# Linear attention mixed with a GEGLU feed-forward block on one core: K and Q of the first four tiles moved ahead of the feed-forward units, with finer loads at the start

## The chip, the cores and the metric

One core of one Trainium2 chip. The metric is the time of one execution in microseconds (us). Engines: PE is the TensorE matmul, PEld its weight load, DVE the VectorE, ACT the ScalarE, POOL the GpSimd, SP the queue that issues most DMA loads. "Clock" below means the rate at which PE takes columns: a 512-column matmul takes 427 ns while it is slow and 216 ns once it is released (spacing of matmul starts in the traces). "Landed" means that the last update of a load's semaphore has come. A bracket on a row of weight loads is idle time of the weight loads; the time that PE itself stands can be shorter (0.31 against 0.64 us in the first profile of the changed kernel).

## The reference

Two branches read the same `x` (2048 tokens, 640 features) and are mixed by a gate:

```python
g = sigmoid((x * gate_w).sum(-1, keepdims=True))
a = linear_attention(x, wqkv) @ wo      # 32 heads of 20; phi(t) = where(t > 0, t + 1, exp(t)) + 1e-6
b = (gelu(x @ w_gate) * (x @ w_up)) @ w_down   # 1728 hidden features
return g * a + (1 - g) * b
```

## The kernel before

Tokens are cut into 16 tiles of 128 and 4 quarters of 512. `xT` is x with features on the partitions; the first quarter is transposed on PE, the others by DMA. The order is: E (feed-forward units, 14 per quarter) of quarter 0; K of all 16 tiles; Q of all tiles with G (x transposed times phi(K)) between them; then the rest of E and the output F. The PSUM pool has 8 buffers, shared by all.

```python
dma(out=x_sb[0][:, 0:2, :], in_=x_view[:, 0:2, :])       # x tiles 0, 1: 320 KB
dma(out=wg[:, :, 0:256], in_=wg_v[:, :, 0:256])          # 320 KB
dma(out=wu[:, :, 0:256], in_=wu_v[:, :, 0:256])          # 320 KB
dma(out=x_sb[0][:, 2:4, :], in_=x_view[:, 2:4, :])       # x tiles 2, 3: 320 KB
# ... the rest of w_gate and w_up, then w_k, gate_w in 2-byte pieces, transposing loads, w_q ...

for r in range(NWARM):                                    # NWARM = 7
    nc.tensor.matmul(t[:], lhsT=ones, rhs=ones, ...)      # warm-up

transpose_x(0)                                            # tiles 0, 1
e01 = [(ps_tile("ps_g"), ps_tile("ps_u")) for _ in range(2)]
for ft in range(2):
    e_mm(e01[ft][0], wg, ft, 0, 0, 256)                   # half a quarter wide
e_mm(e01[0][1], wu, 0, 0, 0, 256)
transpose_x(1)                                            # tiles 2, 3
e_mm(e01[1][1], wu, 1, 0, 0, 256)
for ft in range(2):
    e_mm(e01[ft][0], wg, ft, 0, 256, 256)
    e_mm(e01[ft][1], wu, ft, 0, 256, 256)
    e_out(0, ft, *e01[ft])
for ft in range(2, NF):
    phase_E(0, ft)
for st in range(NT):
    phase_K(st)
# ... Q with G, and the rest ...
```

Of the kernel before, what the change touches and what calls it, by code (L numbers as in the profile page):

```python
# [16 lines left out]
def kernel(  # L17
# [12 lines left out]
    nc = tc.nc  # L30
# [13 lines left out]
    GW = GH * Dh  # L44
    NG = 6
    gw = [min(GW, D - GW * g) for g in range(NG)]
    NWARM = 7

    x2 = A_x[0]
    out2 = out[0]  # L50
# [8 lines left out]
    def ps_tile(name):  # L59
        return psum.tile([P, QW], FP32, name=name, tag="ps")  # L60
# [7 lines left out]
    x_sb = [x_all[:, 4 * q : 4 * q + 4, :] for q in range(NQ)]  # L68
    pk_q = [ov.tile([P, 4, D], BF16, name=f"pk{q}", tag="slab_a", bufs=NQ) for q in range(NQ)]
    pk = [pk_q[t // 4][:, t % 4, :] for t in range(NT)]  # L70
    WQK = 2 * D + 1
    wqk = ov.tile([P, ND, WQK], BF16, name="wqk", tag="slab_c")

    wg = wpool.tile([P, ND, FM], BF16, name="wg")
    wu = wpool.tile([P, ND, FM], BF16, name="wu")
# [10 lines left out]
    nc.gpsimd.memset(ones_bf[:], 1.0)  # L86

    dma = nc.sync.dma_start
    dma(out=x_sb[0][:, 0:2, :], in_=x_view[:, 0:2, :])  # L89
    dma(out=wg[:, :, 0:256], in_=wg_v[:, :, 0:256])  # L90
    dma(out=wu[:, :, 0:256], in_=wu_v[:, :, 0:256])  # L91
    dma(out=x_sb[0][:, 2:4, :], in_=x_view[:, 2:4, :])
    warm = consts.tile([P, 1], FP32, name="act_warm")
    nc.scalar.activation(out=warm[:], in_=nc.const_aps.tensor(1.0, [P, 1], BF16), func=ACT.Gelu_apprx_tanh)
    for lo, hi in ((256, 512), (512, 1024), (1024, FM)):
        dma(out=wg[:, :, lo:hi], in_=wg_v[:, :, lo:hi])
        dma(out=wu[:, :, lo:hi], in_=wu_v[:, :, lo:hi])
    dma(out=wgu[:, :, 0:FL], in_=wg_v[:, :, FM:F])
    dma(out=wgu[:, :, FL:P], in_=wu_v[:, :, FM:F])
    dma(out=wqk[:, :, 0:D], in_=wqkv_v[:, :, D : 2 * D])  # L100
    with nc.allow_non_contiguous_dma(reason="tiny gate_w column load"):
        dma(out=wqk[:, :, D : D + 1], in_=gate_w.rearrange("(k p o) -> p k o", p=P, o=1))
    for q in (1, 2, 3):
        nc.sync.dma_start_transpose(out=xT[q][:, :, :], in_=x2[q * QW : (q + 1) * QW, :])
    dma(out=wqk[:, :, D + 1 : WQK], in_=wqkv_v[:, :, 0:D])
    for q in (1, 2, 3):
        dma(out=x_sb[q][:], in_=x_view[:, 4 * q : 4 * q + 4, :])
    dma(out=wv[:], in_=wqkv_v[:, :, 2 * D : 3 * D])
# [6 lines left out]
    for r in range(NWARM):  # L115
        nc.tensor.matmul(t[:], lhsT=nc.const_aps.tensor(1.0, [P, P], BF16),
                         rhs=nc.const_aps.tensor(1.0, [P, QW], BF16), start=(r == 0), stop=(r == NWARM - 1))

    NGB = 4
    mask = consts.tile([GW, NGB * GW], BF16, name="mask")  # L120
# [12 lines left out]
    eneg = consts.tile([P, NT], FP32, name="eneg")  # L133
    gsc = {}

    def transpose_x(pair):
        t0 = 2 * pair
        tpa = psum.tile([P, 2 * QW], BF16, name="tp_a", tag="ps")
        tpb = psum.tile([P, 2 * QW], BF16, name="tp_b", tag="ps")
        c0 = t0 * P  # L140
        for dk in range(ND):
            tp, o = (tpa, dk * 2 * P) if dk < 2 else (tpb, (dk - 2) * 2 * P)
            for i in range(2):
                nc.tensor.transpose(  # L144
                    tp[:, o + i * P : o + (i + 1) * P], x_sb[0][:, t0 + i, dk * P : (dk + 1) * P], ident[:]
                )
        nc.vector.tensor_copy(
            out=xT[0][:, 0:2, c0 : c0 + 2 * P], in_=tpa[:, 0 : 4 * P].rearrange("p (k n) -> p k n", k=2),
        )
        nc.scalar.copy(  # L150
            out=xT[0][:, 2:3, c0 : c0 + 2 * P], in_=tpb[:, 0 : 2 * P].rearrange("p (k n) -> p k n", k=1),
        )
        nc.vector.tensor_copy(
            out=xT[0][:, 3:5, c0 : c0 + 2 * P], in_=tpb[:, 2 * P : 6 * P].rearrange("p (k n) -> p k n", k=2),
        )

    hT_cur = {}
    hT0 = big.tile([P, NF, QW], BF16, name="hT0")
# [3 lines left out]
    def e_mm(ps, w, ft, q, t0=0, tw=QW):  # L162
        for dk in range(ND):
            nc.tensor.matmul(ps[:, t0 : t0 + tw], lhsT=w[:, dk, ft * P : (ft + 1) * P],  # L164
                             rhs=xT[q][:, dk, t0 : t0 + tw], start=(dk == 0), stop=(dk == ND - 1))

    def e_out(q, ft, psg, psu):
        gl = work.tile([P, QW], BF16, name="gl")
        nc.scalar.activation(out=gl[:], in_=psg[:], func=ACT.Gelu_apprx_tanh)  # L169
        nc.vector.tensor_tensor(out=hT_cur[q][:, ft, :], in0=psu[:], in1=gl[:], op=ALU.mult)  # L170
# [24 lines left out]
            out=dst, in0=src, scalar=0.0, in1=m[:, :width], op0=ALU.max, op1=ALU.add,  # L195
        )

    def proj(ps, st, lo, hi):
        q, sl = divmod(st, 4)
        for dk in range(ND):  # L200
            nc.tensor.matmul(  # L201
                ps[:, 0 : hi - lo], lhsT=xT[q][:, dk, sl * P : (sl + 1) * P],
                rhs=wqk[:, dk, lo:hi], start=(dk == 0), stop=(dk == ND - 1),
            )

    CH = ((0, QW), (QW, D))

    def phase_K(st):
        for lo, hi in CH:
            ps = ps_tile("ps_k")  # L210
            proj(ps, st, lo, hi + (hi == D))
            phi(pk[st][:, lo:hi], ps[:, 0 : hi - lo], hi - lo)
        nc.scalar.activation(
            out=eneg[:, st : st + 1], in_=ps[:, D - QW : D - QW + 1], func=ACT.Exp, scale=-1.0
        )

    def phase_Q(st):
        for lo, hi in CH:
            ps = ps_tile("ps_q")
            proj(ps, st, D + 1 + lo, D + 1 + hi)  # L220
            phi(pq[st][:, lo:hi], ps[:, 0 : hi - lo], hi - lo)

    g_sb = big.tile([P, ND, D], BF16, name="g_sb")
# [19 lines left out]
    def phase_Z(st):  # L243
        if st == 0:
            return
        nc.vector.tensor_tensor(out=(zsum[:] if st == NT - 1 else zacc[:]), in0=(pk[0][:] if st == 1 else zacc[:]),
                                in1=pk[st][:], op=ALU.add)
# [47 lines left out]

    def phase_M(g):
        if g == 0:
            M["all"] = ov.tile([P, ND + NG, D], BF16, name="m_all", tag="slab_c")
        m_sb = M["all"][:, 0:ND, :]
        m_st = M["all"][:, ND : ND + NG, :]  # L300
        for hh in range(2):
            cs = slice(hh * HALF, (hh + 1) * HALF)
            mp = ps_tile("ps_m")
            nc.tensor.matmul(mp[0 : gw[g], 0:HALF], lhsT=kvt[0 : gw[g], g, 0 : gw[g]],  # L304
                             rhs=wo_g[0 : gw[g], g, cs], start=True, stop=True)
            if hh == 0:
                nc.vector.tensor_copy(out=m_st[0 : gw[g], g, cs], in_=mp[0 : gw[g], 0:HALF])
            else:
                nc.scalar.copy(out=m_st[0 : gw[g], g, cs], in_=mp[0 : gw[g], 0:HALF])
        lo = GW * g  # L310
        hi = lo + gw[g]
        while lo < hi:
            k = lo // P
            e = min(hi, (k + 1) * P)
            dma(out=m_sb[lo - k * P : e - k * P, k, :], in_=m_st[lo - GW * g : e - GW * g, g, :])
            lo = e
# [23 lines left out]
    def phase_F(st):  # L340
        q, sl = divmod(st, 4)
        hT = hT_cur[q]
        ts = slice(sl * P, (sl + 1) * P)
        o_out = work.tile([P, D], BF16, name="o_out", bufs=2)
        omg = gsc["omg"][:, st : st + 1]
        parts = ((0, HALF), (HALF, HALF + 160), (HALF + 160, D)) if st == NT - 1 else ((0, HALF), (HALF, D))
        for i, (lo, hi) in enumerate(parts):
            acc = ps_tile("ps_acc")
            for dk in range(ND):
                nc.tensor.matmul(acc[:, 0 : hi - lo], lhsT=pqT[q][:, dk, ts],  # L350
                                 rhs=M["all"][:, dk, lo:hi], start=(dk == 0), stop=False)
            for ft in range(NF):
                nc.tensor.matmul(acc[:, 0 : hi - lo], lhsT=hT[:, ft, ts],  # L353
                                 rhs=wd[:, ft, lo:hi], start=False, stop=(ft == NF - 1))
            if i == 0:
                nc.scalar.activation(out=o_out[:, lo:hi], in_=acc[:, 0 : hi - lo], func=ACT.Copy, scale=omg)  # L356
            else:
                nc.vector.tensor_scalar(out=o_out[:, lo:hi], in0=acc[:, 0 : hi - lo],  # L358
                                        scalar1=omg, scalar2=None, op0=ALU.mult)
            if i == 1:  # L360
                dma(out=out2[st * P : (st + 1) * P, 0:hi], in_=o_out[:, 0:hi])
            elif i == 2:
                dma(out=out2[st * P : (st + 1) * P, lo:hi], in_=o_out[:, lo:hi])

    transpose_x(0)
    e01 = [(ps_tile("ps_g"), ps_tile("ps_u")) for _ in range(2)]
    for ft in range(2):
        e_mm(e01[ft][0], wg, ft, 0, 0, 256)
    e_mm(e01[0][1], wu, 0, 0, 0, 256)
    transpose_x(1)  # L370
    e_mm(e01[1][1], wu, 1, 0, 0, 256)
    for ft in range(2):
        e_mm(e01[ft][0], wg, ft, 0, 256, 256)
        e_mm(e01[ft][1], wu, ft, 0, 256, 256)
        e_out(0, ft, *e01[ft])
    for ft in range(2, NF):
        phase_E(0, ft)

    for st in range(NT):
        phase_K(st)  # L380
    phase_gate()
    gu = g_units()
    done = 0
    total = NT * ND * D
    for st in range(NT):
        phase_Q(st)
        phase_Z(st)
        while done < total * (st + 1) // (NT + 1):
            done += next(gu)
    phase_Zrep()  # L390
    for w in gu:
# [56 lines left out]
```

## Time and profile before

| | |
|---|---|
| time, median of the first 3 runs | 281.02 us (280.21 to 281.13) |
| span of the profiled run | 279.0 us |
| PE busy | 274.2 us, 98% |
| E units of the first quarter from the third on, to the end of the quarter | 11.73 to 36.71 us |

The page of the kernel before: the span, the busy time of each engine, and PE's busy tenths in 40 slices.

```profile
span 279.0 us, 4391 instructions
PE 274.2 (98%) x1738; PEld 157.4 (56%) x1738; DVE 140.5 (50%) x313; ACT 80.0 (29%) x176; POOL 4.5 (2%) x13
PE   8999999999999999999999999999999999999995
```

PE is full in all slices but the first and the last. So only the start has something to give. The timeline of the kernel before, rows of PE and of its weight loads (start us, us, engine, line, operation, out<-in, shapes, count, and in brackets the idle time before and what ended it):

```profile
0.85 3.15 PE L116 MATMUL warm_ps<-const-bfloat16-1.0 128*128 128x512 bf16 x7 [0.85 <-PEq L432]
4.20 0.98 PEld L144 LDWEIGHTS <-x_all 128*128 128x128 bf16 x10 [1.11 <-DMA x_all<-in_A_x_dram]
5.32 1.69 PE L164 MATMUL ps_g<-xT,wg 128*128 128x256 bf16 x10
7.39 0.44 PEld L164 LDWEIGHTS <-wu 128*128 128x128 bf16 x5 [0.65 <-DMA wu<-in_B_w_up_dram]
8.33 0.56 PEld L144 LDWEIGHTS <-x_all 128*128 128x128 bf16 x10 [0.50 <-DMA x_all<-in_A_x_dram]
11.73 1.24 PE L164 MATMUL ps_g<-xT,wg 128*128 128x512 bf16 x5
```

Read it so: ten transposes need 0.98 us of weight loads while the clock is slow (row at 4.20) and 0.56 us once it is released (row at 8.33). PE waits twice for loads. By 11.73 it has done E units 0 and 1, which at full rate are four groups of 1.08 us (5 matmuls of 216 ns), 4.32 us. The start thus costs 11.73 - 4.32 = 7.41 us on top of useful matmuls.

### The profile page before, as it was taken

The page shows a single profiled execution, that of the slowest core. Times are in us where ns is not written, and L with a number is a line of the kernel's source. Part 1 is how long each engine was busy: PE and PEld are TensorE (multiplying, and loading weights), DVE is VectorE, ACT ScalarE, POOL GpSimd, SP SyncE. Part 2 cuts the span into 40 slices and gives each one's busy share as a digit, 9 for nine tenths or more (in the row PEclk, how much of TensorE's full clock was granted, in tenths as well). Part 3 has the DMA queues.
Part 4 walks back from the last instruction along what each step waited for, and adds up shares of the span by engine and source line. Part 5 has one row for each costly group of instructions (what it writes and reads, how often), then busy time and mean ns, then how long its engine had stood idle before and what let it go on. Part 6 is the DMA issues. An engine that isn't in the chain of part 4 may idle for free.

```text
span 279.0 us, 4391 instructions
## 1 busy us (share of the span) xinstructions
PE 274.2 (98%) x1738; PEld 157.4 (56%) x1738; DVE 140.5 (50%) x313; ACT 80.0 (29%) x176; POOL 4.5 (2%) x13
## 2 busy tenths in 40 slices
PE   8999999999999999999999999999999999999995
PEld 4644455554554684544677544457754445777774
DVE  1333259999945469999999532220112332010011
ACT  2322266653433452442200322320022222100100
POOL 5000000000000000000000000000000000000000
PEclk9999999999999999999999999999999999999999
DMA  7999999400000003243223500000100000001001
GB/s 201 338 311 195 270 357 266 149 2 0 0 4 0 0 2 51 47 111 78 49 48 73 142 0 0 2 0 24 43 30 0 2 0 0 26 24 47 26 24 47
DMA packets 35505, 20.83 MB, mean 75 GB/s; under 512 B 21342, under 2 KB 35486, under 8 KB 35486
## 3 DMA queue, kind: packets, MB, share of 16 engines
q1 hardware_dynamic: 35486, 20.57, 28.0%
q8 instruction: 13, 0.21, 0.3%
q14 instruction: 6, 0.05, 0.0%
HBM read 12.54 MB, written 2.62 MB: 54 GB/s over the span
## 4 chain that ended last, share of the span: by engine, by line
PE 96%; DMA 2%; SPq 1%; DVE 0%; issue 0%
PE ps_acc L353 22%; PE ps_u L164 20%; PE ps_g L164 20%; PE ps_k L201 8%; PE ps_q L201 8%; PE ps_acc L350 8%; PE ps_G L230 8%; DMA x_all<-in_A_x_dram 2%; PE ps_gu L164 2%; PE ps_m L304 1%; PE ps_kv L276 1%; SPq L91 0%; SPq L89 0%; SPq L90 0%; PE tp_a L144 0%; DVE o_out L358 0%
## 5 line engine op out<-in xcount | busy, mean ns | idle before, releaser
L353 PE MATMUL ps_acc<-wd,hT 128*128 128x320 bf16 (+1 forms) x462 | 66.3, 295 | 0.0
L164 PE MATMUL ps_u<-xT,wu 128*128 128x512 bf16 (+1 forms) x270 | 65.1, 371 | 0.4 <-DMA wu<-in_B_w_up_dram 0.4
L164 PE MATMUL ps_g<-xT,wg 128*128 128x512 bf16 (+1 forms) x270 | 65.3, 371 | 0.1
L170 DVE TENSOR_TENSOR hT<-ps_u,gl 128x512 bf16<-128x512 f32 x52 | 35.7, 687 | 54.5 <-PE ps_u L164 52.6
L353 PEld LDWEIGHTS <-hT 128*128 128x128 bf16 x462 | 44.5, 98 | 16.5
L169 ACT ACTIVATE gl<-ps_g 128x512 bf16<-128x512 f32 x52 | 31.0, 597 | 72.3 <-PE ps_g L164 71.6
L164 PEld LDWEIGHTS <-wu 128*128 128x128 bf16 x270 | 26.3, 98 | 30.3 <-DMA wu<-in_B_w_up_dram 0.7
L164 PEld LDWEIGHTS <-wg 128*128 128x128 bf16 x270 | 26.1, 98 | 28.5 <-issue 0.7
L201 PEld LDWEIGHTS <-xT 128*128 128x128 bf16 x320 | 25.8, 97 | 22.4
L358 DVE TENSOR_SCALAR o_out<-ps_acc,omg_all 128x320 bf16<-128x320 f32 (+1 forms) x17 | 8.9, 525 | 55.0 <-PE ps_acc L353 53.5
L356 ACT ACTIVATE o_out<-ps_acc,omg_all 128x320 bf16<-128x320 f32 x16 | 8.4, 527 | 70.4 <-PE ps_acc L353 57.1
L350 PE MATMUL ps_acc<-m_all,pqT 128*128 128x320 bf16 (+1 forms) x165 | 27.1, 295 | 0.0
L230 PE MATMUL ps_G<-pk,x_all 128*128 128x512 bf16 (+1 forms) x160 | 24.5, 299 | 0.0
L201 PE MATMUL ps_q<-wqk,xT 128*128 128x512 bf16 (+1 forms) x160 | 24.4, 299 | 0.0
L201 PE MATMUL ps_k<-wqk,xT 128*128 128x512 bf16 (+1 forms) x160 | 22.0, 299 | 0.0
L191 DVE TENSOR_SCALAR phi_m<-phi_e 128x512 bf16<-128x512 bf16 x64 | 12.8, 238 | 14.6 <-ACT phi_e L189 14.4
L350 PEld LDWEIGHTS <-pqT 128*128 128x128 bf16 x165 | 15.9, 98 | 6.4
L189 ACT ACTIVATE phi_e<-ps_q 128x512 bf16<-128x512 f32 (+1 forms) x32 | 12.4, 435 | 21.6 <-PE ps_q L201 19.7
L230 PEld LDWEIGHTS <-x_all 128*128 128x128 bf16 x160 | 11.9, 97 | 6.5
L189 ACT ACTIVATE phi_e<-ps_k 128x512 bf16<-128x512 f32 (+1 forms) x32 | 12.8, 439 | 5.9 <-PE ps_k L201 5.6
L194 DVE SCALAR_TENSOR_TENSOR pq<-ps_q,phi_m 128x512 bf16<-128x512 f32 (+1 forms) x32 | 14.3, 485 | 0.0
L194 DVE SCALAR_TENSOR_TENSOR pk<-ps_k,phi_m 128x512 bf16<-128x512 f32 (+1 forms) x32 | 14.1, 483 | 0.0
(54 smaller groups left out, 114.0 us busy)
## 6 DMA issues: line engine op xcount, KB each, us to landing
out_dram<-o_out SPq DMA_DIRECT2D x15, 160.0 KB, 1.8
wd<-in_B_w_down_dram SPq DMA_DIRECT2D x1, 2080.0 KB, 15.7
x_all<-in_A_x_dram SPq DMA_DIRECT2D x3, 640.0 KB, 7.5
wqk<-in_A_wqkv_dram SPq DMA_DIRECT2D x2, 800.0 KB
wg<-in_B_w_gate_dram SPq DMA_DIRECT2D x1, 800.0 KB, 8.5
wu<-in_B_w_up_dram SPq DMA_DIRECT2D x1, 800.0 KB
wv<-in_A_wqkv_dram SPq DMA_DIRECT2D x1, 800.0 KB, 10.6
wo_g<-in_A_wo_dram SPq DMA_DIRECT2D x1, 750.0 KB
```

What stands on the lines that cost most here:

```text
L164: nc.tensor.matmul(ps[:, t0 : t0 + tw], lhsT=w[:, dk, ft * P : (ft + 1) * P], rhs=xT[q][:, dk, t0 : t0 + tw], start=(dk == 0), stop=(dk == ...
L169: nc.scalar.activation(out=gl[:], in_=psg[:], func=ACT.Gelu_apprx_tanh)
L170: nc.vector.tensor_tensor(out=hT_cur[q][:, ft, :], in0=psu[:], in1=gl[:], op=ALU.mult)
L189: nc.scalar.activation(out=e[:, :width], in_=src, func=ACT.Exp)
L191: nc.vector.tensor_scalar(out=m[:, :width], in0=e[:, :width], scalar1=1.0, scalar2=EPS, op0=ALU.min, op1=ALU.add,)
L194: nc.vector.scalar_tensor_tensor(out=dst, in0=src, scalar=0.0, in1=m[:, :width], op0=ALU.max, op1=ALU.add,)
L201: nc.tensor.matmul(ps[:, 0 : hi - lo], lhsT=xT[q][:, dk, sl * P : (sl + 1) * P], rhs=wqk[:, dk, lo:hi], start=(dk == 0), stop=(dk == ND - 1),)
L230: nc.tensor.matmul(gp[:, 0 : hi - lo], lhsT=x_all[:, st, ct * P : (ct + 1) * P], rhs=pk[st][:, lo:hi], start=(st == 0), stop=(st == NT - 1),)
L350: nc.tensor.matmul(acc[:, 0 : hi - lo], lhsT=pqT[q][:, dk, ts], rhs=M["all"][:, dk, lo:hi], start=(dk == 0), stop=False)
L353: nc.tensor.matmul(acc[:, 0 : hi - lo], lhsT=hT[:, ft, ts], rhs=wd[:, ft, lo:hi], start=False, stop=(ft == NF - 1))
L356: nc.scalar.activation(out=o_out[:, lo:hi], in_=acc[:, 0 : hi - lo], func=ACT.Copy, scale=omg)
L358: nc.vector.tensor_scalar(out=o_out[:, lo:hi], in0=acc[:, 0 : hi - lo], scalar1=omg, scalar2=None, op0=ALU.mult)
```

## The change

The intent: begin with work that needs few bytes, so that PE gets going sooner. K of tiles 0 to 3 is computed first, from single w_k blocks of 160 KB as they land, then Q of those tiles, then E of the quarter. Cut to its core:

```diff
-    NWARM = 7
+    NWARM = 6
+    nc.scalar.dma_start(out=gw5[:], in_=gate_w.rearrange("(k p) -> k p", p=P))   # then transposed on PE
-    dma(out=x_sb[0][:, 0:2, :], in_=x_view[:, 0:2, :])
-    dma(out=wg[:, :, 0:256], in_=wg_v[:, :, 0:256])
-    dma(out=wu[:, :, 0:256], in_=wu_v[:, :, 0:256])
-    dma(out=x_sb[0][:, 2:4, :], in_=x_view[:, 2:4, :])
+    dma(out=x_sb[0][:, 0, :], in_=x_view[:, 0, :])
+    dma(out=wk[:, 0, 0:D], in_=wqkv_v[:, 0, D : 2 * D])
+    dma(out=x_sb[0][:, 1, :], in_=x_view[:, 1, :])
+    for dk in range(1, ND):
+        dma(out=wk[:, dk, 0:D], in_=wqkv_v[:, dk, D : 2 * D])
+        if dk == 1:
+            dma(out=x_sb[0][:, 2:4, :], in_=x_view[:, 2:4, :])
+    dma(out=wq[:], in_=wqkv_v[:, :, 0:D])
-    # gate_w in 2-byte pieces into the column beside w_k (cut)
+    def k_first():
+        transpose_x(0)
+        fill(0, (256,))            # filler matmul, result not used
+        mm(0, 0, 0)                # mm(tile, column part, feature block)
+        transpose_x(1)
+        fill(1, (512, 512))
+        mm(0, 0, 1)
+        mm(1, 0, 0)
+        mm(1, 0, 1)
+        for st in (2, 3):
+            transpose_x(st)
+        for dk in range(2):
+            for st in (2, 3):
+                mm(st, 0, dk)
+        for dk in range(2, ND):
+            for st in range(4):
+                mm(st, 0, dk)
+        # gate column copied into wk by GpSimd; then the narrow column part of each tile, and phi (cut)
+    k_first()
+    for st in range(4):
+        phase_Q(st)
+    for ft in range(NF):
+        phase_E(0, ft)
+    for st in range(4, NT):
+        phase_K(st)
```

Later loops run over tiles 4 to 15 instead of 0 to 15, and the sum over tiles (Z) is spread over 12 steps instead of 16. The weights w_k and w_q become two buffers. Not shown in the cut: x is transposed tile by tile instead of in pairs, with the copies divided anew between VectorE and ScalarE; w_gate and w_up are loaded in three pieces each instead of four; ScalarE loads the table of Exp first instead of that of Gelu.

More of the change, by code (lines that the diff above doesn't have):

```diff
@@ L70 @@
     pk = [pk_q[t // 4][:, t % 4, :] for t in range(NT)]
-    WQK = 2 * D + 1
-    wqk = ov.tile([P, ND, WQK], BF16, name="wqk", tag="slab_c")
+    wk = ov.tile([P, ND, D + 1], BF16, name="wk", tag="slab_c")
+    wq = ov.tile([P, ND, D], BF16, name="wq", tag="slab_d")
     wg = wpool.tile([P, ND, FM], BF16, name="wg")
@@ L88 @@
     dma = nc.sync.dma_start
-    dma(out=x_sb[0][:, 0:2, :], in_=x_view[:, 0:2, :])
-    dma(out=wg[:, :, 0:256], in_=wg_v[:, :, 0:256])
-    dma(out=wu[:, :, 0:256], in_=wu_v[:, :, 0:256])
-    dma(out=x_sb[0][:, 2:4, :], in_=x_view[:, 2:4, :])
+    gw5 = consts.tile([ND, P], BF16, name="gw5")
+    nc.scalar.dma_start(out=gw5[:], in_=gate_w.rearrange("(k p) -> k p", p=P))
[7 more added lines that the diff above has]
+    dma(out=wq[:], in_=wqkv_v[:, :, 0:D])
     warm = consts.tile([P, 1], FP32, name="act_warm")
-    nc.scalar.activation(out=warm[:], in_=nc.const_aps.tensor(1.0, [P, 1], BF16), func=ACT.Gelu_apprx_tanh)
-    for lo, hi in ((256, 512), (512, 1024), (1024, FM)):
+    nc.scalar.activation(out=warm[:], in_=nc.const_aps.tensor(1.0, [P, 1], BF16), func=ACT.Exp)
+    for lo, hi in ((0, 512), (512, 1024), (1024, FM)):
         dma(out=wg[:, :, lo:hi], in_=wg_v[:, :, lo:hi])
@@ L99 @@
     dma(out=wgu[:, :, FL:P], in_=wu_v[:, :, FM:F])
-    dma(out=wqk[:, :, 0:D], in_=wqkv_v[:, :, D : 2 * D])
-    with nc.allow_non_contiguous_dma(reason="tiny gate_w column load"):
-        dma(out=wqk[:, :, D : D + 1], in_=gate_w.rearrange("(k p o) -> p k o", p=P, o=1))
     for q in (1, 2, 3):
         nc.sync.dma_start_transpose(out=xT[q][:, :, :], in_=x2[q * QW : (q + 1) * QW, :])
-    dma(out=wqk[:, :, D + 1 : WQK], in_=wqkv_v[:, :, 0:D])
     for q in (1, 2, 3):
@@ L117 @@
                          rhs=nc.const_aps.tensor(1.0, [P, QW], BF16), start=(r == 0), stop=(r == NWARM - 1))
+    fps = t
+    tg = psum.tile([P, 2 * QW], BF16, name="tp_g", tag="ps")
+    nc.tensor.transpose(tg[:, 0:ND], gw5[:], ident[0:ND, 0:ND])
+    gcol = consts.tile([P, ND], BF16, name="gcol")
+    nc.vector.tensor_copy(out=gcol[:], in_=tg[:, 0:ND])
     NGB = 4
@@ L134, with transpose_x @@
     gsc = {}
-    def transpose_x(pair):
-        t0 = 2 * pair
-        tpa = psum.tile([P, 2 * QW], BF16, name="tp_a", tag="ps")
-        tpb = psum.tile([P, 2 * QW], BF16, name="tp_b", tag="ps")
-        c0 = t0 * P
-        for dk in range(ND):
-            tp, o = (tpa, dk * 2 * P) if dk < 2 else (tpb, (dk - 2) * 2 * P)
-            for i in range(2):
-                nc.tensor.transpose(
-                    tp[:, o + i * P : o + (i + 1) * P], x_sb[0][:, t0 + i, dk * P : (dk + 1) * P], ident[:]
-                )
-        nc.vector.tensor_copy(
-            out=xT[0][:, 0:2, c0 : c0 + 2 * P], in_=tpa[:, 0 : 4 * P].rearrange("p (k n) -> p k n", k=2),
-        )
-        nc.scalar.copy(
-            out=xT[0][:, 2:3, c0 : c0 + 2 * P], in_=tpb[:, 0 : 2 * P].rearrange("p (k n) -> p k n", k=1),
-        )
-        nc.vector.tensor_copy(
-            out=xT[0][:, 3:5, c0 : c0 + 2 * P], in_=tpb[:, 2 * P : 6 * P].rearrange("p (k n) -> p k n", k=2),
-        )
+    def transpose_x(t):
+        ts = slice(t * P, (t + 1) * P)
+        for cp, lo, hi in ((nc.vector.tensor_copy, 0, 2), (nc.scalar.copy, 2, ND)):
+            tp = psum.tile([P, 2 * QW], BF16, name="tp_x", tag="ps")
+            for dk in range(lo, hi):
+                o = (dk - lo) * P
+                nc.tensor.transpose(tp[:, o : o + P], x_sb[0][:, t, dk * P : (dk + 1) * P], ident[:])
+            cp(out=xT[0][:, lo:hi, ts], in_=tp[:, 0 : (hi - lo) * P].rearrange("p (k n) -> p k n", n=P))
     hT_cur = {}
@@ L196, in phi, with proj @@
         )
-    def proj(ps, st, lo, hi):
+    def proj(ps, w, st, lo, hi):
         q, sl = divmod(st, 4)
@@ L202, in proj, with k_out, phase_K, fill @@
                 ps[:, 0 : hi - lo], lhsT=xT[q][:, dk, sl * P : (sl + 1) * P],
-                rhs=wqk[:, dk, lo:hi], start=(dk == 0), stop=(dk == ND - 1),
+                rhs=w[:, dk, lo:hi], start=(dk == 0), stop=(dk == ND - 1),
             )
     CH = ((0, QW), (QW, D))
-    def phase_K(st):
-        for lo, hi in CH:
-            ps = ps_tile("ps_k")
-            proj(ps, st, lo, hi + (hi == D))
+    def k_out(st, pss):
+        for (lo, hi), ps in zip(CH, pss):
             phi(pk[st][:, lo:hi], ps[:, 0 : hi - lo], hi - lo)
         nc.scalar.activation(
-            out=eneg[:, st : st + 1], in_=ps[:, D - QW : D - QW + 1], func=ACT.Exp, scale=-1.0
+            out=eneg[:, st : st + 1], in_=pss[1][:, D - QW : D - QW + 1], func=ACT.Exp, scale=-1.0
         )
+    def phase_K(st):
+        pss = [ps_tile("ps_k") for _ in CH]
+        for (lo, hi), ps in zip(CH, pss):
+            proj(ps, wk, st, lo, hi + (hi == D))
+        k_out(st, pss)
+    def fill(t, cols):
+        for w in cols:
+            nc.tensor.matmul(fps[:, 0:w], lhsT=ident[:], rhs=x_sb[0][:, t, 0:w], start=True, stop=True)
+    def k_first():
+        pss = [[ps_tile("ps_k")] for _ in range(4)]
+        def mm(st, c, dk):
+            lo, hi = CH[c]
+            hi += hi == D
+            nc.tensor.matmul(
+                pss[st][c][:, 0 : hi - lo], lhsT=xT[0][:, dk, st * P : (st + 1) * P],
+                rhs=wk[:, dk, lo:hi], start=(dk == 0), stop=(dk == ND - 1),
+            )
+        transpose_x(0)
[14 more added lines that the diff above has]
+                mm(st, 0, dk)
+        for dk in range(ND):
+            nc.gpsimd.tensor_copy(out=wk[:, dk, D : D + 1], in_=gcol[:, dk : dk + 1])
+        for st in range(4):
+            pss[st].append(ps_tile("ps_k"))
+            for dk in range(ND):
+                mm(st, 1, dk)
+            k_out(st, pss[st])
     def phase_Q(st):
@@ L219, in phase_Q @@
             ps = ps_tile("ps_q")
-            proj(ps, st, D + 1 + lo, D + 1 + hi)
+            proj(ps, wq, st, lo, hi)
             phi(pq[st][:, lo:hi], ps[:, 0 : hi - lo], hi - lo)
@@ L297, in phase_M @@
         if g == 0:
-            M["all"] = ov.tile([P, ND + NG, D], BF16, name="m_all", tag="slab_c")
-        m_sb = M["all"][:, 0:ND, :]
-        m_st = M["all"][:, ND : ND + NG, :]
+            M["sb"] = ov.tile([P, ND, D], BF16, name="m_sb", tag="slab_c")
+            M["st"] = ov.tile([GW, NG, D], BF16, name="m_st", tag="slab_d")
+        m_sb, m_st = M["sb"], M["st"]
         for hh in range(2):
@@ L350, in phase_F @@
                 nc.tensor.matmul(acc[:, 0 : hi - lo], lhsT=pqT[q][:, dk, ts],
-                                 rhs=M["all"][:, dk, lo:hi], start=(dk == 0), stop=False)
+                                 rhs=M["sb"][:, dk, lo:hi], start=(dk == 0), stop=False)
             for ft in range(NF):
@@ L363, in phase_F @@
                 dma(out=out2[st * P : (st + 1) * P, lo:hi], in_=o_out[:, lo:hi])
-    transpose_x(0)
-    e01 = [(ps_tile("ps_g"), ps_tile("ps_u")) for _ in range(2)]
-    for ft in range(2):
-        e_mm(e01[ft][0], wg, ft, 0, 0, 256)
-    e_mm(e01[0][1], wu, 0, 0, 0, 256)
-    transpose_x(1)
-    e_mm(e01[1][1], wu, 1, 0, 0, 256)
-    for ft in range(2):
-        e_mm(e01[ft][0], wg, ft, 0, 256, 256)
-        e_mm(e01[ft][1], wu, ft, 0, 256, 256)
-        e_out(0, ft, *e01[ft])
-    for ft in range(2, NF):
+    k_first()
+    for st in range(4):
+        phase_Q(st)
+    for ft in range(NF):
         phase_E(0, ft)
-    for st in range(NT):
+    for st in range(4, NT):
         phase_K(st)
@@ L384 @@
     total = NT * ND * D
-    for st in range(NT):
+    for st in range(4, NT):
         phase_Q(st)
-        phase_Z(st)
-        while done < total * (st + 1) // (NT + 1):
+        for z in range(4 * (st - 4) // 3, 4 * (st - 3) // 3):
+            phase_Z(z)
+        while done < total * (st - 3) // (NT - 3):
             done += next(gu)
```

## The prediction

> **What bounds the kernel now.** The page gives PE 274.2 us busy of a 279.0 us span; the chain of waits is 96% PE. By stages (windows view) PE is busy without a break from 10 us on: first E quarter 11.7 to 36.7, K to 58.6 (21.86 us for 16 tiles, 1.37 each), Q with G to 102.2; the waits view has no PE wait after 8.4 us. So only the start can give anything. There (timeline, 0 to 12 us): seven warm-up matmuls fill PE to 4.0; the first x tiles land at 4.2; ten transposes take until 5.3; ten 256-column matmuls run to about 6.8 with pauses for transposed copies; PE waits for w_up until 7.39 and for x tiles 2 and 3 until 8.33 (weight loads idle 0.65 and 0.50 us). At 11.73 the 40 half-width matmuls are done, worth 4.4 us at the 110 ns spacing seen later. The start costs 11.73 - 4.4 = 7.3 us beyond useful matmuls, 1.65 of it transposes that stay.
>
> **What the change does.** K of the first four tiles comes first, fed by 160 KB loads of x and w_k; then Q of those tiles, then E. Useful matmul work is unchanged. It removes the two waits and the scattered 2-byte gate load, which held up nothing on PE. It adds three filler matmuls, a gate transpose, small GpSimd copies, and one activation table load (1.28 us on ACT, which is 29% busy).
>
> Estimate of the new start, from the trace's durations: x tile 0 is half the first load and lands near 3.6 us. PE is still slow then: the Trainium skill, "TensorE: Matmul & The Clock Gate", Part 1, puts the release after about 3.4 us of activity, with spacing N/1.2 GHz before; the trace agrees (warm-up weight loads 427 ns apart, first transposes 107, later ones 56). I take the release at 5.3 to 5.8 us. From 3.6: five transposes 0.54, short filler 0.21, one K matmul 0.43, five transposes 0.5, two fillers 0.4 to 0.85, three K matmuls 0.65, perhaps 0.3 waiting for x or copies, ten transposes 0.57, sixteen K matmuls at 216 ns 3.45, twenty narrow ones 1.15. That ends near 11.8 to 12. Useful in it is 4 x 1.37 = 5.5 us, so the start costs 6.4 instead of 7.3. The last w_k block should land near 8 us (eight loads issued 0.52 us apart, 300 to 350 GB/s, completion 1 to 2 us behind), before PE needs it: the start is bound by PE work.
>
> Then eight tiles of phi pass through DVE at 1.28 us a tile against PE's 1.37, with 8 PSUM banks: little margin; I allow 0.2 us of stall. Later stages stay PE-bound and do not move.
>
> **Prediction.** Gain 0.7 us net: 280.3 us, range 279.0 to 281.6. Faster by over 2%: 0.02; within 2%: 0.95; slower: 0.03.
>
> **What would show it.** Right: x tile 0's transposes start near 3.6 us; PE waits on w_k are short; K of four tiles done near 12 us; later stages as long as before. Wrong: PE waiting for w_k (DMA-bound start), the clock still slow after 7 us, or PE waiting for PSUM at the first Q tiles.
>
> **What would make it wrong.** A later clock release (each us at half rate costs 0.5 us); small loads landing later than large ones; a stall behind DVE or ACT in the K burst (1 to 2 us slower); or much earlier landing (1 us faster).

## More of the kernel before

The chain of waits of the kernel before, in its first 12 us (start us, us, what):

```profile
2.38 5.91 DMA x_all<-in_A_x_dram
8.29 0.05 issue
8.34 0.40 PE tp_a L144 x4
```

The link that ends last in the start is the load of x tiles 2 and 3, which lands at 8.29.

## The result, and the profile after

The changed kernel takes 280.33 us (median of 12 runs, 279.88 to 281.29) against 281.02 for the kernel before (15 runs, 279.99 to 283.54). The ratio is 0.9979, with a 95% interval of 0.9959 to 0.9999: within 2%, 0.7 us between the medians. Ratios here are the mean time of one kernel's fast runs over the mean of the other's fast runs of the same rounds, so they are not quite the ratios of the medians. One run of the kernel before took 283.54 us; without it the means differ by 0.4 us.

The page of the changed kernel, and then its timeline for PE and the weight loads:

```profile
span 277.8 us, 4366 instructions
PE 274.0 (99%) x1721; PEld 155.7 (56%) x1721; DVE 139.7 (50%) x314; ACT 82.0 (30%) x179; POOL 5.2 (2%) x18
```

```profile
3.61 0.45 PEld L150 LDWEIGHTS <-x_all 128*128 128x128 bf16 x5
4.12 0.42 PE L219 MATMUL warm_ps<-x_all,ident 128*128 128x256 bf16 x1
4.72 0.37 PEld L150 LDWEIGHTS <-x_all 128*128 128x128 bf16 x5 [0.23 <-DMA x_all<-in_A_x_dram]
5.11 0.59 PE L219 MATMUL warm_ps<-x_all,ident 128*128 128x512 bf16 x2
5.54 0.81 PE L227 MATMUL ps_k<-wk,xT 128*128 128x512 bf16 x3
6.49 0.56 PEld L150 LDWEIGHTS <-x_all 128*128 128x128 bf16 x10 [0.64 <-DMA x_all<-in_A_x_dram]
7.17 4.77 PE L227 MATMUL ps_k<-wk,xT 128*128 128x512 bf16 x36
17.39 1.24 PE L160 MATMUL ps_g<-xT,wg 128*128 128x512 bf16 x5
```

Tile 0 is transposed from 3.61 instead of 4.20. Five transposes take 0.45 us of weight loads slow, 0.28 fast; the row at 4.72 with 0.37 lies between, so the clock was released near 4.9. Then the weight loads stand idle for 0.64 us until x tiles 2 and 3 land. PE itself waits less: its three K matmuls from 5.54 take 0.65 us at 216 ns each, to 6.19, and the transposes begin at 6.50, so it stands 0.31 us. By the semaphore updates in the packed trace, w_k blocks 2, 3 and 4 landed at 6.83, 7.87 and 8.47 us, and the first matmuls that need them began at 8.04, 8.91 and 9.77: each had 1.0 to 1.3 us to spare.

The chain of waits of the changed kernel in its first 12 us:

```profile
2.67 3.77 DMA x_all<-in_A_x_dram
6.50 0.73 PE tp_x L150 x10
7.23 4.71 PE ps_k L227 x36
11.94 0.33 PE ps_q L197
```

Again the load of x tiles 2 and 3 is the last link of the waiting. It has 0.98 MB of loads up to its own end instead of 1.31 MB, and it lands at 6.44 instead of 8.29. From there on PE runs on with no wait for a load. K of the four tiles is done at 11.94; at the steady rate (16 tiles in 21.86 us before) these four are worth 5.46 us, so the start costs 6.48 us instead of 7.41. That is 0.93 us less.

Where did the 1.85 us of earlier landing go? In the kernel before, 15 half-width matmuls (three of the eight groups, about 1.62 us at full rate) were done while waiting for x tiles 2 and 3. In the changed kernel only 4 matmuls of 216 ns, 0.86 us, are done by then. So 0.76 us of the gain is work that now comes after the landing instead of before it; what is left is about 1.1, near the 0.93 found.

Later stages, by the windows view (stretch and length, then busy time of PE, PEld, DVE, ACT, POOL, clock, DMA share, GB/s): first 16 K tiles of the kernel before, then 12 K tiles of the changed one.

```profile
36.71:58.57 21.86, 21.86 (x162) 12.33 (x160) 19.69 (x63) 14.76 (x46) 0.00 (x0) 1.00 0.75 217
```

```profile
46.69:63.08 16.39, 16.39 (x122) 9.25 (x120) 14.29 (x45) 11.42 (x34) 0.00 (x0) 1.00 0.34 115
```

Both are 1.366 us per tile. The equal point of both kernels shows the same: eight K/Q tiles plus all of E of the first quarter are done at 46.69 in the changed kernel, and would be at 36.71 + 8 x 1.366 = 47.64 in the kernel before. From that point to the end the changed kernel is only about 0.2 us shorter, so nearly all of the difference between these two profiles lies in the start.

### The profile page after: what moved, and what is told of

Its sections match the earlier page's. It is cut to its first block, busy times and chain, and to the rows that moved or that the text cites. A ratio compares the mean times of both kernels' runs of the same rounds, so it can differ in the third digit from the quotient of the medians.

```text
span 277.8 us, 4366 instructions
## 1 busy us (share of the span) xinstructions
PE 274.0 (99%) x1721; PEld 155.7 (56%) x1721; DVE 139.7 (50%) x314; ACT 82.0 (30%) x179; POOL 5.2 (2%) x18
## 4 chain that ended last, share of the span: by engine, by line
PE 97%; DMA 1%; SPq 1%; DVE 0%; issue 0%
PE ps_acc L392 22%; PE ps_g L160 20%; PE ps_u L160 20%; PE ps_q L197 8%; PE ps_acc L389 8%; PE ps_G L269 8%; PE ps_k L197 6%; PE ps_k L227 2%; PE ps_gu L160 2%; DMA x_all<-in_A_x_dram 1%; PE ps_m L343 1%; PE ps_kv L315 1%; PE tp_x L150 0%; SPq L95 0%; SPq L93 0%; SPq L92 0%
## 5 line engine op out<-in xcount | busy, mean ns | idle before, releaser
L160 PE MATMUL ps_g<-xT,wg 128*128 128x512 bf16 x260 | 64.6, 379 | 0.0
L160 PE MATMUL ps_u<-xT,wu 128*128 128x512 bf16 x260 | 64.6, 379 | 0.0
L160 PEld LDWEIGHTS <-wu 128*128 128x128 bf16 x260 | 25.5, 98 | 30.7
L160 PEld LDWEIGHTS <-wg 128*128 128x128 bf16 x260 | 25.2, 98 | 28.8 <-issue 0.3
L197 PEld LDWEIGHTS <-xT 128*128 128x128 bf16 x280 | 22.6, 98 | 19.3
L389 PE MATMUL ps_acc<-m_sb,pqT 128*128 128x320 bf16 (+1 forms) x165 | 27.1, 295 | 0.0
L197 PE MATMUL ps_q<-wq,xT 128*128 128x512 bf16 (+1 forms) x160 | 23.9, 299 | 0.0
L269 PE MATMUL ps_G<-pk,x_all 128*128 128x512 bf16 (+1 forms) x160 | 23.9, 299 | 0.0
L197 PE MATMUL ps_k<-wk,xT 128*128 128x512 bf16 (+1 forms) x120 | 16.6, 299 | 0.0
## 6 DMA issues: line engine op xcount, KB each, us to landing
wg<-in_B_w_gate_dram SPq DMA_DIRECT2D x1, 800.0 KB, 10.7
```

Source lines behind the costliest of these rows:

```text
L160: nc.tensor.matmul(ps[:, t0 : t0 + tw], lhsT=w[:, dk, ft * P : (ft + 1) * P], rhs=xT[q][:, dk, t0 : t0 + tw], start=(dk == 0), stop=(dk == ...
L197: nc.tensor.matmul(ps[:, 0 : hi - lo], lhsT=xT[q][:, dk, sl * P : (sl + 1) * P], rhs=w[:, dk, lo:hi], start=(dk == 0), stop=(dk == ND - 1),)
L269: nc.tensor.matmul(gp[:, 0 : hi - lo], lhsT=x_all[:, st, ct * P : (ct + 1) * P], rhs=pk[st][:, lo:hi], start=(st == 0), stop=(st == NT - 1),)
L389: nc.tensor.matmul(acc[:, 0 : hi - lo], lhsT=pqT[q][:, dk, ts], rhs=M["sb"][:, dk, lo:hi], start=(dk == 0), stop=False)
```

## The experiments

Three theories were held against each other. W: the start is the sum of PE work, as the prediction had it. D: the w_k loads bind it. X: the landing of x tiles 2 and 3 ends the waiting part. For every variant of the changed kernel the table gives the start of the first E unit and the span of the profiled run, and the ratio to the kernel before.

| variant | E starts, us | span, us | span - start | ratio to before (95%) |
|---|---|---|---|---|
| changed kernel | 17.39 | 277.8 | 260.4 | 0.9979 (0.9959 to 0.9999) |
| changed kernel, again | 18.47 | 278.9 | 260.4 | 0.9986 (0.9969 to 1.0003) |
| no fillers | 18.14 | 278.5 | 260.4 | 0.9978 (0.9962 to 0.9994) |
| no warm-up | 17.81 | 278.2 | 260.4 | 1.0002 (0.9976 to 1.0027) |
| x loads first | 17.43 | 277.9 | 260.5 | 0.9994 (0.9977 to 1.0011) |
| x tiles 2, 3 later | 18.81 | 279.2 | 260.4 | 1.0032 (1.0004 to 1.0060) |
| x tiles 0, 1 in one load | 18.11 | 278.5 | 260.4 | 0.9991 (0.9975 to 1.0007) |
| x tiles 2, 3 singly | 18.12 | 278.6 | 260.5 | 1.0007 (0.9991 to 1.0023) |
| w_q ahead of w_k blocks | 19.35 | 279.7 | 260.4 | 1.0042 (1.0018 to 1.0066) |
| alternating loads | 17.93 | 278.4 | 260.5 | 1.0000 (0.9983 to 1.0016) |
| the same, w_q in two parts | 18.69 | 279.2 | 260.5 | 0.9991 (0.9970 to 1.0012) |

The fourth column is the main finding: whatever is done to the start, the time from the first E unit to the end is 260.4 to 260.6 us (260.38 to 260.55 with unrounded times). In these variants the start of E alone decides the time. It also shows that the same kernel differs by 1.1 us between two profiled runs (17.39 and 18.47). One profile of the start is therefore one draw; the waits inside it can be read exactly, but its total must not be compared with another's as if it were a mean. The first profile of the changed kernel is in fact the fastest of its 12 runs (279.88 us). The spans of the 12 are 277.8 to 279.2 us, median 278.25; less the constant, E began near 17.9 us in the median run. That is an estimate; by it the start costs about 6.9 us in the median run, not 6.48.

### Without the fillers

```diff
-        fill(0, (256,))
-        fill(1, (512, 512))
```

> The changed kernel without its three filler matmuls. In the profile after the change the chain of waits runs through the load of x tiles 2 and 3 (landing 6.44 us), and PE is idle before it for 0.64 us. Theory X (the start ends with that load): the fillers lie in time that PE would wait anyway; transposes of tiles 2 and 3 start at 6.4 to 6.6 us as before, K of four tiles ends at 11.9 +- 0.2, unless the clock is released later, which would add up to 0.5 us per us. Theory W (the start is the sum of PE work, as the prediction had it): 0.4 to 0.6 us earlier, about 11.4.

The timeline rows of this run where the waiting ends:

```profile
7.25 0.56 PEld L150 LDWEIGHTS <-x_all 128*128 128x128 bf16 x10 [1.47 <-DMA x_all<-in_A_x_dram]
7.92 4.77 PE L227 MATMUL ps_k<-wk,xT 128*128 128x512 bf16 x36
```

In this run x tiles 2 and 3 landed 0.8 us later than in the first profile, with the same loads ahead of them, so the expected 11.9 was missed (12.69). But the work after the landing took 5.44 us, as in the changed kernel (6.49 to 11.94, 5.45). PE was done with its earlier work at about the same time as with fillers (its last K matmul before the transposes began at 5.90, there at 5.97), because the clock came later, at 5.6 instead of 4.85 us; most of the longer wait is the later landing. PE itself then stood 1.1 us, as long as the three fillers would take even at the slow rate (1.07 us), so here they would have cost nothing. The timed runs are as fast as with fillers. That speaks for X; the interval alone does not quite exclude the small end of W's 0.4 us.

### Without the warm-up

```diff
-    NWARM = 6
+    NWARM = 0
```

> The changed kernel without the six warm-up matmuls, so that PE is idle until 3.5 us. If the clock is released by activity: transposes and the first K matmuls stay at the slow spacing (107 and 427 ns) until about 7 to 9 us, and K of four tiles ends 0.3 to 1.5 us later than 11.9, because some of the 5.4 us of work after x tiles 2 and 3 runs at half rate. If warming is not needed: no change.

Weight loads of the last early K matmuls and of the transposes of tiles 2 and 3:

```profile
5.90 0.15 PEld L227 LDWEIGHTS <-xT 128*128 128x128 bf16 x1 [0.28 <-issue]
6.33 0.10 PEld L227 LDWEIGHTS <-xT 128*128 128x128 bf16 x1 [0.28 <-issue]
6.91 0.56 PEld L150 LDWEIGHTS <-x_all 128*128 128x128 bf16 x10 [0.48 <-DMA x_all<-in_A_x_dram]
```

The clock was slow until 6.33 (0.43 us between matmuls) and fast from there on, earlier than the 7 to 9 us expected. PE had been active from 2.6 us on. K ended at 12.36, 0.4 us later, but that much is also the later landing in this run (transposes at 6.91 instead of 6.49). Four timed runs spread from 280.30 to 281.98, and the ratio of 1.0002 against 0.9978 without fillers in the same call suggests a loss of about 0.7 us; the intervals overlap.

### All x tiles first

```diff
-    # x0, wk0, x1, wk1, x2 and x3 together, wk2, wk3, wk4; fillers
+    for i in range(4):
+        dma(out=x_sb[0][:, i, :], in_=x_view[:, i, :])
+    for dk in range(ND):
+        dma(out=wk[:, dk, 0:D], in_=wqkv_v[:, dk, D : 2 * D])
...
+        for st in range(4):
+            transpose_x(st)
+        for dk in range(ND):
+            for st in range(4):
+                mm(st, 0, dk)
```

> The changed kernel with the loads of x tiles 0 to 3 (singly) ahead of all w_k blocks, all 20 transposes first, no fillers, then four K matmuls per w_k block. Theory X: x tile 3 lands near 5.0 to 5.5, transposes run from 3.6 to about 5.7 (partly at the slow clock), first K matmuls near 6.0, K of four tiles ends at 10.4 to 11.0: 0.9 to 1.5 us faster than the changed kernel in the stage, total about 279.1. Theory D (the landing of w_k blocks binds): the last block lands near 8 as now; the end is then set by 8 + 0.9 + 1.2 = 10.1 or later, with PE waits on w_k in between. Theory W: PE work from 3.6 less the fillers, 11.3 to 11.5.

Timeline and weight loads of this run:

```profile
5.73 0.45 PEld L147 LDWEIGHTS <-x_all 128*128 128x128 bf16 x5 [0.60 <-DMA x_all<-in_A_x_dram]
6.25 5.72 PE L224 MATMUL ps_k<-wk,xT 128*128 128x512 bf16 x40
11.98 5.43 PEld L194 LDWEIGHTS <-xT 128*128 128x128 bf16 x40 [0.19 <-DMA wq<-in_A_wqkv_dram]
```

The times of X and W were missed, and the waits for w_k that D expected did not appear: K ended at 11.97. Tile 3 landed at 5.7, and the clock was still slow then (0.45 us for five). With all transposes ahead of all K matmuls, nothing useful was left to do before that landing, so the whole of K, 5.7 us, came after it. w_q landed at 11.94 us, just as K ended: it cost PE nothing in this run, but it would have been the next limit.

### x tiles first, in the kernel before

```diff
-    dma(out=x_sb[0][:, 0:2, :], in_=x_view[:, 0:2, :])
+    for i in range(4):
+        dma(out=x_sb[0][:, i, :], in_=x_view[:, i, :])
-    dma(out=x_sb[0][:, 2:4, :], in_=x_view[:, 2:4, :])      # after w_gate and w_up
...
+    for i in range(4):
+        transpose_x(i)                                       # tile by tile
+    for ft in range(NF):
+        phase_E(0, ft)                                       # all at full width; E stays first
```

> The kernel before, with E still first, only with x tiles 0 to 3 loaded singly ahead of w_gate and w_up, transposed first, and all E units at full width. If the order of loads at the start matters and the move of K to the front does not: the third E unit starts at 10.4 to 10.8 instead of 11.73, gain 0.9 to 1.3 us over before, as much as or more than the change gave. If moving K to the front is what helps: no gain over before.

```profile
6.94 0.76 PEld L152 LDWEIGHTS <-wg 128*128 128x128 bf16 x5 [0.94 <-DMA wg<-in_B_w_gate_dram]
11.27 1.24 PE L152 MATMUL ps_g<-xT,wg 128*128 128x512 bf16 x5
```

The third unit starts at 11.27 instead of 11.73: half of the expected gain in this profile, the fastest of the six runs, since the weight loads now wait 0.94 us for the first w_gate block. The timed runs fall into two groups, 280.28 to 280.42 (three) and 281.88 to 283.65 (three), and the ratio of 1.0023 (0.9987 to 1.0058) says nothing. Whether moving K to the front is needed, or whether a better load order with E first would do as well, stays open.

### The load of x tiles 2 and 3 later

```diff
-        if dk == 1:
+        if dk == 3:
             dma(out=x_sb[0][:, 2:4, :], in_=x_view[:, 2:4, :])
```

> The changed kernel with the load of x tiles 2 and 3 issued two w_k blocks later (after block 3 instead of after block 1), all else the same. Theory X (that load's landing ends the waiting part of the start): it lands 0.8 to 1.0 us later and K of four tiles ends as much later, about 12.8; total about +0.9 us over the changed kernel. Theory W (the start is the sum of PE work): PE has slack there, at most +0.3.

```profile
7.90 0.56 PEld L150 LDWEIGHTS <-x_all 128*128 128x128 bf16 x10 [1.60 <-DMA x_all<-in_A_x_dram]
8.58 4.77 PE L227 MATMUL ps_k<-wk,xT 128*128 128x512 bf16 x35
```

The transposes began at 7.90, 1.4 us later than in the first profile of the changed kernel, and K ended at 13.35, 1.4 us later. Against the two runs in which the load in its old place landed later (the run without fillers and the repeat below), it is 0.7 us. The ratio rose from 0.998 to 1.0032, about 1.4 us; one run of six, 283.54 us at a clock of 0.994, carries part of that, and by the medians it is 1.2 us. This is X's answer; W's limit of 0.3 is exceeded by every one of these figures. The expected delay was 0.8 to 1.0.

### x tiles 0 and 1 in one load

```diff
-    dma(out=x_sb[0][:, 0, :], in_=x_view[:, 0, :])
+    dma(out=x_sb[0][:, 0:2, :], in_=x_view[:, 0:2, :])
-    dma(out=x_sb[0][:, 1, :], in_=x_view[:, 1, :])
```

> The changed kernel with x tiles 0 and 1 in one load of 320 KB, as in the kernel before; all else the same. First transposes move from 3.6 to 4.0 to 4.3 us. Theory W and the prediction's step (x tile 0's earlier landing is cashed in): K of four tiles ends 0.4 to 0.6 us later. Theory X: PE only waits less before x tiles 2 and 3, which land as before; end of K unchanged within 0.2 us.

PE in this run, the two long fillers first:

```profile
5.53 1.06 PE L218 MATMUL warm_ps<-x_all,ident 128*128 128x512 bf16 x2
6.38 1.01 PE L226 MATMUL ps_k<-wk,xT 128*128 128x512 bf16 x3
7.22 0.72 PE L149 MATMUL tp_x<-ident,x_all 128*128 128x128 bf16 x10
```

There is no wait for a load before the transposes at 7.22: tiles 2 and 3 had landed at 6.88. The two fillers took 0.43 us each (5.53 to 6.38), the three K matmuls 0.84 together (to 7.22): one slow, two fast. PE was late because the clock was released only near 6.8, although the six warm-up matmuls were the same as in the changed kernel, where it was released near 4.9. First transposes moved only 0.2 us, to 3.81. K ended at 12.66. So here the path was PE work at the slow rate, and the fillers lay on it: W holds when the clock comes late. With the load landed at 6.88, leaving the fillers out could have saved 0.3 us at most; that was not run. The run does not tell what x tile 0's landing is worth, because the clock moved with it.

### x tiles 2 and 3 singly

```diff
-            dma(out=x_sb[0][:, 2:4, :], in_=x_view[:, 2:4, :])
+            for i in (2, 3):
+                dma(out=x_sb[0][:, i, :], in_=x_view[:, i, :])
...
-        fill(1, (512, 512))
...
         for st in (2, 3):
             transpose_x(st)
-        for dk in range(2):
-            for st in (2, 3):
+            for dk in range(2):
                 mm(st, 0, dk)
```

> The changed kernel with x tiles 2 and 3 in single loads, each transposed and given its two K matmuls as it lands, and without the two 512-wide fillers. Theory X: x tile 2 lands near 5.8, tile 3 near 6.3, and the work of tile 2 fills the wait for tile 3; K of four tiles ends 0.3 to 0.6 us earlier, 11.4 to 11.6; total about 0.4 us under the changed kernel. If single loads do not land earlier than the pair: no gain.

```profile
7.13 1.02 PE L228 MATMUL ps_k<-wk,xT 128*128 128x512 bf16 x4 [0.65 <-DMA wk<-in_A_wqkv_dram]
12.67 5.43 PEld L198 LDWEIGHTS <-xT 128*128 128x128 bf16 x40 [0.68 <-DMA wq<-in_A_wqkv_dram]
```

The expectation failed for a reason outside the theories. The instruction order that was built differs from the source: K matmuls that need w_k block 2 were put ahead of the transposes of tile 3, and PE stood at block 2 until 7.13 although tile 3 had landed at 6.33. Later it waited for w_q as well. What single loads would give in the intended order is not tested by this run.

### w_q ahead of w_k blocks 2 to 4

```diff
             dma(out=x_sb[0][:, 2:4, :], in_=x_view[:, 2:4, :])
+            dma(out=wq[:], in_=wqkv_v[:, :, 0:D])
-    dma(out=wq[:], in_=wqkv_v[:, :, 0:D])
```

> The changed kernel with the 800 KB load of w_q moved ahead of w_k blocks 2 to 4, which then land about 2.3 us later (block 4 near 10.2 instead of 7.9). If the w_k blocks have slack as the prediction said (block 4 is needed near 9.9, block 2 near 8.2): K of four tiles ends 0.3 to 0.9 us later. If the start is bound by the w_k loads: the full 2.3 us later.

```profile
6.28 1.01 PE L227 MATMUL ps_k<-wk,xT 128*128 128x512 bf16 x3
10.00 3.89 PE L227 MATMUL ps_k<-wk,xT 128*128 128x512 bf16 x31 [1.18 <-DMA wk<-in_A_wqkv_dram]
```

K ended at 13.9, 1.95 us later than in the first profile: between the two expectations, which were 0.3 to 0.9 and 2.3. Of this, 1.18 us is the wait for block 2; most of the rest is a late clock again (near 6.7: the first of the three K matmuls from 6.28 was still slow, and the transposes began 0.6 us later than in the first profile). Block 2 landed at 9.96 us here, 3.1 us later than in the first profile (6.83), where it was needed at 8.04. So it had 1.2 us to spare there, and the later blocks 1.0 and 1.3: the w_k loads did not bind the start.

### Alternating single loads, without fillers; and w_q in two parts

```diff
-    NWARM = 6
+    NWARM = 5
-    # x0, wk0, x1, wk1, x2 and x3 together, wk2, wk3, wk4
+    # x0, x1, wk0, x2, wk1, x3, wk2, wk3, wk4
+        transpose_x(0)
+        for i in range(1, 4):
+            transpose_x(i)
+            for st in range(i):
+                mm(st, 0, i - 1)
+            for dk in range(i):
+                mm(i, 0, dk)
+        for dk in (3, 4):
+            for st in range(4):
+                mm(st, 0, dk)
```

and, in the second version, `wq[:, :, 0:512]` and `wq[:, :, 512:D]` as two loads.

> A version built to beat both. In all profiles so far the span is the start of E plus 260.4 us (within 0.1), so the start alone decides. x tiles and w_k blocks are loaded alternately and singly, each landing is given its own K matmuls, there are no fillers and five warm-up matmuls. Theory X: no single landing holds PE for long; the last w_k block lands near 8.0 and K of four tiles ends near 11.1 instead of 11.9. Then Q may wait for w_q, which landed near 12 in the run with x first (PE waited 0.2 us there): in that case Q starts near 12 and nothing is gained over the changed kernel.

> As the alternating version, with w_q loaded in two column parts (512, then 128 columns). If w_q's landing is the next limit: the first part lands about 0.6 us earlier than the whole did, Q starts near 11.4, E near 16.9, total about 0.4 us under the changed kernel. If not: like the alternating version without the split.

Weight loads of the first version, then of the second:

```profile
12.49 5.44 PEld L196 LDWEIGHTS <-xT 128*128 128x128 bf16 x40 [0.88 <-DMA wq<-in_A_wqkv_dram]
```

```profile
7.29 0.15 PEld L227 LDWEIGHTS <-xT 128*128 128x128 bf16 x1 [0.28 <-issue]
7.72 0.15 PEld L150 LDWEIGHTS <-x_all 128*128 128x128 bf16 x1 [0.28 <-issue]
8.15 0.47 PEld L150 LDWEIGHTS <-x_all 128*128 128x128 bf16 x4 [0.28 <-issue]
```

In the first version the weight loads were ready for Q at about 11.6 and waited 0.88 us for w_q (PE itself 0.70), as feared. In the second that wait is gone, but in the profiled run, the slowest of its six, the clock was still slow at 8.15, so K took longer. Its timed runs range from 280.12 to 281.68. Neither version is shown to beat the changed kernel (1.0000 and 0.9991 against 0.9986 in the same call).

### The changed kernel again

> The changed kernel again, unchanged, on the same chip as the alternating versions. If the time after the start of E is constant, its span is the start of E plus 260.4 us again, whatever the start was; the start of E between 17.3 and 18.2 us, depending on the landing of x tiles 2 and 3 and on when the clock is released. Ratio to before 0.997 to 0.999.

```profile
5.30 0.28 PEld L150 LDWEIGHTS <-x_all 128*128 128x128 bf16 x5 [0.80 <-DMA x_all<-in_A_x_dram]
7.18 0.56 PEld L150 LDWEIGHTS <-x_all 128*128 128x128 bf16 x10 [0.80 <-DMA x_all<-in_A_x_dram]
13.02 0.11 PEld L197 LDWEIGHTS <-xT 128*128 128x128 bf16 x2 [0.57 <-DMA wq<-in_A_wqkv_dram]
```

The clock was fast by 5.30, but x tiles 2 and 3 landed at 7.14 instead of 6.45, and then Q waited for w_q until 13.02 (PE itself 0.40 us). The chain view names VectorE's `pk` before Q here, but that instruction ended at 13.03, when the weight load had already begun; w_q landed at 12.98, and at 10.72 in the first profile. The start of E at 18.47 lies outside the expected 17.3 to 18.2; the constant of 260.4 us held. So even the unchanged kernel has another last link in another run.

The packed trace shows something of how a landing moves. Each of these loads makes 16 updates of its semaphore. For x tiles 2 and 3 in the run without fillers, 15 had come by 6.19 us and the last came at 7.20; in the first profile these were 6.24 and 6.45. A single late part can thus hold up a whole load; why it was late is not known.

### The compact load of gate_w alone, in the kernel before

```diff
-        dma(out=wqk[:, :, D : D + 1], in_=gate_w.rearrange("(k p o) -> p k o", p=P, o=1))
+    dma(out=gw5[:], in_=gate_w.rearrange("(k p) -> k p", p=P))
+    # before K: transposed on PE, copied into wqk by GpSimd
```

> The kernel before with one part of the change alone: gate_w loaded as five rows and transposed on PE instead of in 2-byte pieces. The prediction said that the scattered load held up nothing on PE: same time as before within 0.1% and no PE wait gone. If it held up the transposing loads or K: up to 0.5 us faster.

```profile
8.01 0.44 PEld L164 LDWEIGHTS <-wu 128*128 128x128 bf16 x5 [1.77 <-DMA wu<-in_B_w_up_dram]
8.93 0.56 PEld L144 LDWEIGHTS <-x_all 128*128 128x128 bf16 x10 [0.47 <-DMA x_all<-in_A_x_dram]
```

No gain: the ratio is 1.0021 (1.0001 to 1.0041), outside the 0.1% that was expected. The span of 279.8 is 0.8 us over that of the kernel before. Of this, 0.6 us is there already at the third E unit (12.32 against 11.73), where the two kernels have run the same instructions and only the clock's release (4.4 instead of 5.2 us) and the landings differ (transposes of x tiles 2 and 3 at 8.93 instead of 8.33; of the 16 parts of that load 15 had come by 7.92 us, the last at 8.88). The K stage is 21.96 instead of 21.86 us. That the scattered load held up nothing on PE is borne out, as the waits view had it; whether the compact form itself costs 0.1 us or the difference is chance is not settled.

## Why the prediction was right, and where a step of it was not

The repeat in this table is the second profile of the changed kernel.

| step of the prediction | predicted | measured in the profile after |
|---|---|---|
| only the start can give anything | stages as long as before | 260.4 us after the start of E in all variants |
| first transposes | 3.6 us | 3.61 us |
| release of the clock | 5.3 to 5.8 us | 4.85 us in this run; 4.7 to 6.8 with the same warm-up |
| waiting for x tiles or copies | 0.3 us | PE: 0.31 us for x tiles 2 and 3, 0.17 us for copies; about 1.6 us in all in the repeat |
| K of four tiles done | 11.8 to 12 us | 11.94 us; 12.63 in the repeat |
| cost of the start | 6.4 us | 6.48 us; 7.56 in the repeat |
| stall of the first Q tiles | 0.2 us | none: Q took 5.45 us, 1.36 a tile; 0.40 us for w_q in the repeat |
| time | 280.3 us | 280.33 us |

The main reading held: PE was full everywhere else, the useful work was unchanged, and the start had only about 7.3 us of cost, so a rearranged start could not give much. The sum of durations then gave the right size.

One step was wrong as it stood: "the start is bound by PE work". In the profile after, the chain of waits runs through the load of x tiles 2 and 3; moving that load later moved the end of K with it (5.45 us from the transposes to the end in both), and taking PE work away (the fillers) changed nothing that the runs can tell. In the first profile the sum still fits almost term by term. PE itself stood 0.31 us for that load, where 0.3 was allowed for all waiting. The five transposes of tile 1 took 0.31 us instead of 0.5 because the clock came early, which paid for the 0.17 us of copies.

But that profile is the fastest of 12 runs. In the repeat the waits add up to about 1.6 us (0.5 for x tile 1, 0.5 for x tiles 2 and 3, 0.4 for w_q, the rest for copies), and E begins 1.08 us later. That the terms agree so well with the profile is therefore partly luck, and so is the agreement of the median to 0.03 us, which is far closer than the runs agree with each other. The prediction gave the term for the waiting no spread of its own, and it is this term that moves most.

What comes last differs from run to run: the landing of x tiles 2 and 3 in the first profile and without fillers, PE work at the slow rate with x tiles 0 and 1 in one load, w_q as well in the repeat. The w_k loads took no part in the changed kernel. That removing one limit meets the next is a likely reason why none of the rearranged versions was shown to beat the changed kernel, but the runs do not show it for each of them.

The prediction's use of the Trainium skill ("TensorE: Matmul & The Clock Gate", Part 1) was sound on the two rates: N/1.2 GHz slow (0.43 us between 512-column matmuls in the run without warm-up) and about half of that once released. It was not sound to assume one moment of release. The same page says that the activity window is free-running and that the point varies; the traces agree and show it varying more than assumed here (4.7 to 6.8 us with the same six warm-up matmuls).

The small gain over before (0.7 us by the medians of the first set, 0.5 by those of the second, 0.4 by the means once the run of 283.54 us is left out) is of the size of the spread between runs of the same kernel (280.08 to 280.95 in six runs of the changed kernel). Over two sets the ratio came out at 0.9979 and 0.9986; only the first interval leaves out 1, and barely.

## What to carry to other kernels

When a kernel is PE-bound except for its start, compute the cost of the start (time to a landmark, less the useful matmuls done by then) before changing it: it caps the gain. Zoom the chain of waits to the start and look for the one load that every path runs through; work that PE does while it would wait for that load is free, as the fillers were here. Look for it in several profiles, because the last load need not be the same. When several limits end together, test on the time after the landmark as well as on the total, and take more than one profile, because landings (w_q: 10.7 and 13.0 us in two runs of the same kernel) and the clock's release (4.7 to 6.8 us) move by up to two microseconds from run to run.

## What the Trainium skill lacked or had wrong

- "TensorE: Matmul & The Clock Gate", Part 1, gives the release of the clock as around 4 us into sustained activity, plus or minus 500 ns. With the same six warm-up matmuls from 0.85 us on and pauses of PE under 0.6 us, it came between 4.7 and 6.8 us in nine runs, 3.8 to 5.9 us into the activity (4.85 in the first profile, 6.8 with x tiles 0 and 1 in one load); with five of them and a pause of 0.9 us it was still slow at 8.15 us. That spread is wider than plus or minus 500 ns; it fits within the window of about 3.4 us that the same section gives.
- "ScalarE: Activation LUTs", "What ACT_TABLE_LOAD costs", gives about 2.66 us for a switch of tables, 1283 ns of load and 1380 ns of drain. Here the load took 1.28 us, but from the end of the last Gelu (36.75 + 0.59 = 37.34) to the start of the first Exp (38.65) only 1.31 us passed; no drain of that size shows. The timeline of ACT in the kernel before:

```profile
36.75 0.59 ACT L183 ACTIVATE gl<-ps_gu 64x512 bf16<-64x512 f32 x1 [1.56 <-PE ps_gu L164]
37.36 1.28 ACT L189 ACT_TABLE_LOAD   x1
38.65 1.43 ACT L189 ACTIVATE phi_e<-ps_k 128x512 bf16<-128x512 f32 x4
```

- No page (as far as read here, "DMA: Bandwidth & Descriptors" in particular) says how much the landing of one load varies from run to run with the same loads ahead of it: x tiles 2 and 3, issued at 2.67 us, let the transposes start at 6.49, 7.18 and 7.25 us in three runs with the same loads. That is as large as the whole effect of this change.
